# Sliding-window attention feeding a mixture of eight experts: q and k held eight tokens to a partition instead of six, the decay mask computed on the chip, and the second and third batch loaded and turned in another order

## The chip, the cores and the metric

The kernel runs on one core of a Trainium2 chip. The metric is the device time of one execution, in microseconds. PE is the matrix engine, PEld its weight loads, DVE the vector engine, ACT the scalar engine, POOL the general engine (here it mostly issues converting DMAs), SP the engine that issues plain DMAs.

## The reference, cut to what matters

```python
# q, k, v: (8 batches, 8 heads, 576 tokens, 64), float32
scores = q @ k.T / 8
rel    = pos[:, None] - pos[None, :]
mask   = (rel >= 0) & (rel < 128)
scores = where(mask, scores - slope[h] * abs(rel), -1e9)     # slope[h] = 2 ** -(h + 1)
x      = softmax(scores) @ v          # (4608 tokens, 512)
P      = exp(x @ w_gate)              # (4608, 8 experts)
for _ in range(8):                    # Sinkhorn: rows, then columns
    P /= P.sum(1); P /= P.sum(0); P *= 4608 / 8
out    = sum(P[:, e:e+1] * (relu(x @ w1[e]) @ w2[e]) for e in range(8))   # w1 512x1024, w2 1024x512
```

## The kernel before, in words

**Loading and turning.** All inputs are float32 in memory and become float16 on the way in, so they come through POOL's queue. `load_qk(b)` (L159) issues four loads for a batch, k and q of heads 0 to 3 and of heads 4 to 7, into tiles `kf`, `qf` with a ring of four buffers. `RT` is 6: a partition holds six consecutive tokens, 96 partitions hold the 576. `turn` (L184) reorders such a tile on DVE into `kp` or `qp`, and `tr_unit` (L194) transposes one pair of heads: `RT` PE transposes of 96 columns each into PSUM (`psT`), then one copy that puts the tokens back into their natural order, on ACT for k (`KT`, L208) and on DVE for q (`QT`, L213). `load_v` (L172) brings v of a batch in five pieces into `vsb_80` or `vsb_81`.

**Attention.** A batch has five key blocks (`kb` 0 to 4; 128 tokens, the last 64), so there are 40 blocks. For each half of the heads `scores` (L218) makes the scores of a key block against up to 256 queries on PE (`psS`), ACT takes the exponential (`pt`, L238), and DVE multiplies by the decay mask (L246). The mask `maskT` is a 512 KB constant (head by 256 queries) that SP's queue loads at the start (L363). The block after it, `attend` (L255) multiplies by v (`psN`), DVE normalises into `xsb` (L286, L287), and `put_x` (L313) transposes that into `xT`. `gates` makes the gate logits.

**Order.** All of it is written out by hand under a manual schedule, so each engine runs its list in order. The loop is at L406. Units of `tr_unit` for the next batch are spread over a block; the loop says when:

```python
                if b == 0:
                    if kb >= 3:
                        units = [(1, nm, 2 * kb - 6 + n) for n in (0, 1) for nm in ("k", "q")]
                elif kb >= 1 and b + 1 < B:
                    units = [(b + 1, nm, kb - 1) for nm in ("k", "q")]
```

For batch 0 the next batch is turned at the ends of `kb` 2 and 3; for every other batch `turn(b + 1, ..., "k")` stands ahead of the first mask of `kb` 0 and 2. Expert 0 needs no routing weight before it is scaled, so its work for the first 24 of 36 token blocks is mixed into the attention loop: `fill` takes pieces of it (L117 first layer, L135 second layer) at 2.85 per block, from the first 512 finished tokens on.

**After the attention.** The Sinkhorn loop (L485) runs on DVE and POOL while PE does the remaining first-layer work of expert 0. Then come expert 1 (nine units of 512 tokens, the loop at L904, `h` 0 to 8) and the experts 2 to 7 in pairs, with Strassen products in both layers (`l1_product` L653, `Unit.product` L760). In expert 1's units `set_apart` (L526) scales a quarter of expert 0's result into a tile `c` (L532) and stores it to `out` through `store_from` (L69, L73) on SP. The tile comes from a ring `st` of five buffers that also serves `m5` (L688) and the staging tiles of `gather_far` (L780, L781); ACT's write of the next `c` waits until both stores of the one before have landed. In the last pass `put_row` (L810) stores finished rows, `add_out` (L817) adds a block's second half into `out` by an accumulating DMA of POOL, and the last unit stores its last rows from ACT's and SP's queues. Loads of later experts' weights (1 MB each as float16) are issued by POOL, the first two in units 1 and 2 of expert 1.

Of the kernel before, what the change touches and what calls it, by code (L numbers as in the profile page):

```python
# [9 lines left out]
FP16 = mybir.dt.float16  # L10
# [4 lines left out]
def kernel(  # L15
# [20 lines left out]
    P = 128  # L36
# [4 lines left out]
    GT = 512  # L41
    NG = Ntok // GT
    NPR = H // 2
    RT = 6
    RATE = 2.85
    RP = S // RT
    scale = float(1.0 / np.sqrt(Dh))

    slopes = 2.0 ** (-8.0 * (np.arange(H, dtype=np.float64) + 1.0) / H)
    _tok = np.arange(2 * P)  # L50
    _kr = np.arange(P)[:, None, None]
    _jq = _tok[None, None, :]
    _rel = _jq - _kr
    maskT_np = np.where(
        (_rel >= 0) & (_rel < P), np.exp(-slopes[None, :, None] * _rel), 0.0
    ).astype(np.float16)
    maskT_h = nc.inline_tensor(maskT_np, name="maskT_c")
    identf_h = nc.inline_tensor(np.eye(P, dtype=np.float32), name="identf_c")
    ident_h = nc.inline_tensor(np.eye(P, dtype=np.float16), name="ident_c")

# [5 lines left out]
    def acc(blk: int):  # L66
        return acc_lo[:, blk, :] if blk < NHI else accs[1][:, blk - NHI, :]

    def store_from(t, blk: int, c0: int, c1: int, engs=(nc.sync,), **kw):  # L69
        n = P // len(engs)  # L70
        for c, eng in enumerate(engs):
            t0 = P * blk + n * c
            eng.dma_start(out=out[t0 : t0 + n, c0:c1], in_=t[n * c : n * c + n], **kw)  # L73

    def store(blk: int, c0: int = 0, c1: int = HD, engs=(nc.sync,)):
        store_from(acc(blk)[:, c0:c1], blk, c0, c1, engs)

    P_sb = per.tile([P, NBLK, E], FP32, name="P_sb")
# [9 lines left out]
    def load_w1(e: int, pool, parts: int = 1):  # L88
        w1ts[e] = pool.tile([P, NDT, Fd], FP16, name=f"w1t_{e}", tag=f"w1{e % 3}", bufs=1)
        w1v = moe_w1[e].rearrange("(dt p) f -> p dt f", p=P)  # L90
        n = Fd // parts
        for c in range(parts):
            nc.gpsimd.dma_start(
                out=w1ts[e][:, :, n * c : n * c + n], in_=w1v[:, :, n * c : n * c + n]
            )
# [50 lines left out]
    with (  # L146
# [12 lines left out]
        def load_qk(b: int):  # L159
            for half in range(2):  # L160
                h0 = 4 * half
                for nm, src in (("k", k), ("q", q)):
                    t = asb.tile(
                        [RP, 4, RT * Dh], FP16, name=f"{nm}f_{b}_{half}", tag="qkf", bufs=4
                    )
                    nc.gpsimd.dma_start(
                        out=t,
                        in_=src[b, h0 : h0 + 4].rearrange("h (p r) d -> p h (r d)", r=RT),
                    )
                    raw[(nm, b, half)] = t  # L170

        def load_v(b: int, kbs=range(NKB)):  # L172
            vsb = vsbs[b % 2]
            for kb in kbs:
                k0 = kb * P
                nk = min(P, S - k0)
                nc.gpsimd.dma_start(  # L177
                    out=vsb[0:nk, kb, :, 0:Dh],
                    in_=v[b, :, k0 : k0 + nk, :].rearrange("h s d -> s h d"),
                )  # L180
# [13 lines left out]
        def tr_unit(b: int, nm: str, j: int):  # L194
            jj = j % 2
            tt = turned[nm]
            psT = aps.tile([P, RT, RP], FP16, name=f"psT_{nm}_{b}_{j}", tag="pmm", bufs=4)
            for r in range(RT):
                nc.tensor.matmul(  # L199
                    out=psT[:, r, :],  # L200
                    lhsT=tt[:, r, 2 * Dh * jj : 2 * Dh * jj + 2 * Dh],
                    rhs=ident[0:RP, 0:RP],
                    is_transpose=True,
                    start=(r == 0),
                    stop=(r == RT - 1),
                )
            if nm == "k":
                nc.scalar.copy(  # L208
                    out=KTs[b % 2][:, j, :].rearrange("p (i r) -> p i r", r=RT),
                    in_=psT.rearrange("p r i -> p i r"),  # L210
                )
            else:
                nc.vector.tensor_copy(  # L213
                    out=QTs[b % 2][:, j, :].rearrange("p (i r) -> p i r", r=RT),
                    in_=psT.rearrange("p r i -> p i r"),
                )

        def scores(b: int, kb: int, half: int):  # L218
# [141 lines left out]
        with tc.manual_schedule():  # L360
            nc.sync.dma_start(out=ident, in_=ident_h.ap())
            load_qk(0)
            nc.sync.dma_start(out=maskT, in_=maskT_h.ap())  # L363
            for vsb in vsbs:
                nc.vector.memset(vsb[:, :, :, Dh : Dh + 2], 1.0)
            load_v(0, range(NKB - 1))
            load_w1(0, per, 2)
            nc.gpsimd.dma_start(
                out=wg_sb, in_=moe_w_gate.rearrange("(dt p) e -> p dt e", p=P)
            )  # L370
            load_v(0, range(NKB - 1, NKB))
            load_qk(1)
            load_w2(0, per)
            load_v(1)

            blocks = [(b, kb) for b in range(B) for kb in range(NKB)]
            pts: dict = {}
            groups = 0
            turn(0, 0, "k")
            turn(0, 0, "q")  # L380
            for j in range(2):
                tr_unit(0, "k", j)
                tr_unit(0, "q", j)

            def finish(i: int):
                b, kb = blocks[i]
                return attend(b, kb, pts[i], pts[i - 1] if kb > 0 else None)

            def finish2(i: int, xsb):
                nonlocal groups  # L390
                b, kb = blocks[i]
                put_x(b, kb, xsb)
                done = b * S + min(S, (kb + 1) * P)
                while (groups + 1) * GT <= done:
                    nc.sync.dma_start(
                        out=x_dram(groups), in_=xT[:, :, GT * groups : GT * groups + GT]
                    )
                    if groups in (NHI // 4, NHI // 4 + 1):
                        load_x(f"0_{groups}", groups)
                    add_group(groups)  # L400
                    groups += 1
                return done

            xsbs: dict = {}
            done = 0
            for i, (b, kb) in enumerate(blocks):  # L406
                units = []
                if b == 0:
                    if kb >= 3:
                        units = [(1, nm, 2 * kb - 6 + n) for n in (0, 1) for nm in ("k", "q")]  # L410
                elif kb >= 1 and b + 1 < B:
                    units = [(b + 1, nm, kb - 1) for nm in ("k", "q")]
                credit = min(credit + RATE, 6.0) if groups else 0.0
                pt0, mask0 = scores(b, kb, 0)
                if i == 0:
                    turn(0, 1, "k")
                    turn(0, 1, "q")
                    for j in range(2, 4):
                        tr_unit(0, "k", j)
                        tr_unit(0, "q", j)  # L420
                if i > 2:
                    gates(done)
                if i > 1:
                    done = finish2(i - 2, xsbs.pop(i - 2))
                for u in units[: len(units) // 2]:
                    tr_unit(*u)
                fill(1)
                turning = kb in (0, 2) and 0 < b < B - 1
                if turning:
                    turn(b + 1, kb // 2, "k")  # L430
                mask0()
                pt1, mask1 = scores(b, kb, 1)
                pts[i] = (pt0, pt1)
                if i > 0:
                    xsbs[i - 1] = finish(i - 1)
                mask1()
                fill(2)
                for u in units[len(units) // 2 :]:
                    tr_unit(*u)
                fill(1)  # L440
                if turning:
                    turn(b + 1, kb // 2, "q")
                if b == 0 and kb in (2, 3):
                    turn(1, kb - 2, "k")
                    turn(1, kb - 2, "q")
                if kb == 0 and b >= 1 and b + 1 < B:
                    load_v(b + 1)
                if kb == 3 and b + 2 < B:
                    load_qk(b + 2)
            i = len(blocks) - 1  # L450
            credit = 1e9
            xsbs[i] = finish(i)
            gates(done)
            done = finish2(i - 1, xsbs[i - 1])
            fill(2)
            gates(done)
            done = finish2(i, xsbs[i])
            fill(1 << 20)
            gates(done)
# [7 lines left out]
    with (  # L467
# [348 lines left out]

        def add_out(blk):  # L817
            store_from(
                acc(blk)[:, HF:HD], blk, HF, HD, (nc.gpsimd,), accum_op=ALU.add
            )  # L820

        def make_x(j, part):
# [265 lines left out]
```

## Time and profile before

| | |
|---|---|
| median of three runs | 1035.37 us (1033.54 to 1036.13) |
| the profiled execution: its time, its span | 1036.13 us, 1034.4 us |
| granted clock | 0.995 |
| PE, PEld busy | 999.3 us (97%), 810.6 us (78%) |
| DVE, ACT, POOL busy | 825.2 us (80%), 647.8 us (63%), 214.6 us (21%) |
| DMA | 128.06 MB; POOL's queue 60.58 MB, 42.9% of 16 engines' span; SP's 65.79 MB, 20.1% |

The busy time of PE in some stretches (us from the span's start):

| stretch | PE busy | DVE | ACT | what runs |
|---|---|---|---|---|
| 0 to 10 | 1.13 | 1.44 | 1.92 | first loads |
| 10 to 20 | 6.47 | 6.11 | 5.59 | batch 0 |
| 20 to 30 | 8.21 | 8.02 | 5.65 | batch 0, second batch turned |
| 30 to 40 | 7.59 | 6.75 | 4.98 | end of batch 0, begin of batch 1 |
| 40 to 50 | 9.81 | 7.16 | 6.32 | batch 1, first work of expert 0 |
| 50 to 60 | 10.00 | 5.87 | 6.30 | the same |
| 200 to 220 (20 us) | 17.77 | 14.82 | 9.00 | Sinkhorn |
| 1020 to 1035 (15 us) | 8.70 | 8.56 | 0.00 | last sums and stores |

In the lines of the timeline a row gives the start, the duration, the engine, the line, the operation, output<-input, the shapes, the count, and in brackets how long the engine stood idle before it and what ended that. Rows of several like instructions are merged. A matmul's end is modelled, so its pitch is read from the starts. SPq, ACTq and POOL rows of DMA_DIRECT2D are issues, not transfers.

### The profile page before, as it was taken

What the parts mean: (1) busy time and instruction counts of PE and PEld (TensorE: products, weight loads), DVE (VectorE), ACT (ScalarE), POOL (GpSimd) and SP (SyncE); (2) the same over time, 40 slices, a digit from 0 to 9 for tenths busy, and PEclk for the clock granted to TensorE, in tenths of its full rate; (3) what the DMA queues carried; (4) which work ended last, traced back from release to release, by engine and by line L of the source; (5) the groups of instructions that cost most, each with busy time, mean ns of one, the idle gap of its engine ahead of it and who ended that gap; (6) DMA issues with size and microseconds to landing.
All of it is one profiled execution on the core that took longest, in us unless ns stands there. A gap on an engine that the chain in (4) does not pass through costs nothing. (4 is left out here: it accounts for less than half of the span.)

```text
span 1034.4 us, 22423 instructions
## 1 busy us (share of the span) xinstructions
PE 999.3 (97%) x9195; PEld 810.6 (78%) x9195; DVE 825.2 (80%) x1282; ACT 647.8 (63%) x1176; POOL 214.6 (21%) x224
## 2 busy tenths in 40 slices
PE   4899999899999999999999999999999999999997
PEld 2555555445888878888888888888888888888886
DVE  4766666576899978877888998888789988888886
ACT  4576767556999856655666656666556665565652
POOL 6332230020322321111112211111111112222222
PEclk9999999999999999999999999999999999999999
DMA  9978893193697794434336964344446635555546
GB/s 177 186 93 99 113 100 54 61 193 102 149 206 154 149 181 102 113 93 93 92 93 133 181 127 101 93 106 110 103 101 136 132 93 133 134 142 148 140 103 133
DMA packets 127078, 128.06 MB, mean 124 GB/s; under 512 B 44128, under 2 KB 104704, under 8 KB 126976
## 3 DMA queue, kind: packets, MB, share of 16 engines
q0 software_dynamic: 94784, 60.58, 42.9%
q1 hardware_dynamic: 31872, 65.79, 20.1%
q8 instruction: 72, 1.18, 0.4%
q10 hardware_dynamic: 320, 0.26, 0.1%
q14 instruction: 30, 0.25, 0.1%
HBM read 113.62 MB, written 16.66 MB: 126 GB/s over the span
## 5 line engine op out<-in xcount | busy, mean ns | idle before, releaser
L117 PEld LDWEIGHTS <-w1t_100 128*128 128x128 f16 x288 | 27.1, 101 | 28.7 <-issue 5.4
L653 PEld LDWEIGHTS <-w1t_3233 128*128 128x128 f16 x288 | 28.1, 98 | 5.9 <-issue 2.5
L653 PEld LDWEIGHTS <-w1t_3215 128*128 128x128 f16 x288 | 28.2, 98 | 5.8 <-issue 1.3
L653 PEld LDWEIGHTS <-w1t_7818 128*128 128x128 f16 x288 | 28.2, 98 | 5.4 <-issue 2.1
L653 PEld LDWEIGHTS <-w1t_7989 128*128 128x128 f16 x288 | 28.1, 98 | 4.3 <-issue 0.3
L653 PEld LDWEIGHTS <-w1t_5152 128*128 128x128 f16 x288 | 28.2, 98 | 3.7 <-issue 0.3
L653 PEld LDWEIGHTS <-w1t_10754 128*128 128x128 f16 x288 | 28.2, 98 | 3.6 <-issue 0.3
L653 PEld LDWEIGHTS <-w1t_3970 128*128 128x128 f16 x256 | 25.0, 98 | 2.9
L177 POOL DMA_DIRECT2D vsb_81<-in_v_dram x20 | 17.3, 871 | 25.4 <-PE psN_4_885 L278 5.2
L177 POOL DMA_DIRECT2D vsb_80<-in_v_dram x20 | 17.6, 889 | 17.9 <-PE psN_4_1287 L278 5.6
L230 PEld LDWEIGHTS <-KT_76 64*128 64x128 f16 (+1 forms) x160 | 6.0, 100 | 15.8 <-issue 13.3
L497 POOL PARTITION_ALL_REDUCE ca_sb<-cs_sb x8 | 3.2, 395 | 63.1 <-DVE cs_sb L494 63.1
L230 PEld LDWEIGHTS <-KT_77 64*128 64x128 f16 (+1 forms) x160 | 5.3, 97 | 13.8 <-issue 12.6
L539 ACT ACTIVATE acc_lo<-acc_lo,Pe_sb 128x512 f32<-128x512 f32 (+1 forms) x24 | 14.8, 615 | 0.0
L73 POOL DMA_DIRECT2D out_dram<-acc_lo x12 | 13.5, 1526 | 0.0
L303 PEld LDWEIGHTS <-xT 128*128 128x128 f16 x144 | 6.1, 98 | 7.4 <-issue 4.9
L781 POOL DMA_DIRECT2D acc_lo<-st_1_0_3813 x1 | 1.2, 1243 | 37.3 <-ACT st_1_0_3813 L780 37.3
L199 PE MATMUL psT_k_0_124<-ident,kp_0_120 96*128 96x96 f16 x6 | 0.7, 278 | 8.2 <-DVE kp_0_120 L188 8.2
L653 PEld LDWEIGHTS <-ws_1_3529 128*128 128x128 f16 x72 | 6.9, 97 | 1.7 <-DVE xd_0_3537 L612 0.6
L653 PEld LDWEIGHTS <-ws_2_4288 128*128 128x128 f16 x72 | 7.0, 98 | 1.5 <-issue 0.7
L808 DVE TENSOR_TENSOR acc_lo<-acc_lo 128x512 f32<-128x512 f32 x12 | 7.7, 684 | 0.0
L73 POOL DMA_DIRECT2D out_dram<-acc_hi x6 | 5.7, 1575 | 9.7 <-DVE acc_hi L771 9.7
(4167 smaller groups left out, 3574.7 us busy)
## 6 DMA issues: line engine op xcount, KB each, us to landing
xTd<-xT SPq DMA_DIRECT2D x9, 512.0 KB, 3.2
out_dram<-acc_lo SPq DMA_DIRECT2D x12, 256.0 KB, 5.7
vsb_80<-in_v_dram POOLq DMA_DIRECT2D x16, 128.0 KB, 7.8
vsb_81<-in_v_dram POOLq DMA_DIRECT2D x16, 128.0 KB, 4.4
out_dram<-acc_lo SPq DMA_DIRECT2D x12, 128.0 KB, 4.6
out_dram<-acc_lo POOLq DMA_DIRECT2D x12, 128.0 KB, 7.5
w1t_100<-in_moe_w_dram POOLq DMA_DIRECT2D x2, 512.0 KB, 10.9
w2t_113<-in_moe_w_dram POOLq DMA_DIRECT2D x1, 1024.0 KB, 14.1
```

What stands on the lines that cost most here:

```text
L73: eng.dma_start(out=out[t0 : t0 + n, c0:c1], in_=t[n * c : n * c + n], **kw)
L117: nc.tensor.matmul(out=psh, lhsT=w1t[:, dt, P * ft : P * ft + P], rhs=x[:, dt, :], start=(dt == 0), stop=(dt == NDT - 1),)
L177: nc.gpsimd.dma_start(out=vsb[0:nk, kb, :, 0:Dh], in_=v[b, :, k0 : k0 + nk, :].rearrange("h s d -> s h d"),)
L199: nc.tensor.matmul(out=psT[:, r, :], lhsT=tt[:, r, 2 * Dh * jj : 2 * Dh * jj + 2 * Dh], rhs=ident[0:RP, 0:RP], is_transpose=True, start=(r ...
L230: nc.tensor.matmul(out=ps[0:nk, hh, jj, 0:nq], lhsT=KT[rows, 2 * half + jj, k0 : k0 + nk], rhs=QT[rows, 2 * half + jj, k0 : k0 + nq],)
L303: nc.tensor.matmul(out=psG, lhsT=xT[:, dt, P * blk : P * blk + P], rhs=wg_sb[:, dt, :], start=(dt == 0), stop=(dt == NDT - 1),)
L497: nc.gpsimd.partition_all_reduce(ca_sb, cs_sb, P, bass_isa.ReduceOp.add)
L539: nc.scalar.mul(acc(blk)[:, c], acc(blk)[:, c], Pe_sb[:, 0, blk : blk + 1])
L653: nc.tensor.matmul(out=ps[:, f, :], lhsT=a[:, kt, f0 : f0 + P], rhs=b[:, kt, :], start=(m in (1, 5) and f == 0 and kt == 0), stop=(kt == 1 ...
L781: nc.gpsimd.dma_start(out=quad(self.g, rh, ch), in_=st, accum_op=ALU.add)
L808: tt(out=t, in0=t, in1=quad(g, 1, 1), op=ALU.add)
```

## The change

- `RT` is 8: a partition holds eight consecutive tokens, 72 partitions hold a batch, a unit is eight PE transposes of 72 columns. k is put back into natural order as before. q is not: within 64 tokens, position 8r + i holds token 8i + r, so that its copy reads and writes runs of eight elements. The mask, `xT`, the results and the rows of `acc` follow that order, and every store to `out` undoes it: its destination is a pattern of 8 by 8 rows, and a store of 128 rows becomes two of 64.
- The 512 KB mask is gone. A 64 KB table of distances (60000 outside the window) is loaded, and ACT makes the mask from it by eight exponentials of 128 x 256, four after the first half's exponential of the first block and four after the second's.
- At the start the order on POOL's queue is v of batch 0 whole, the gate weights, q and k of batch 1, expert 0's first layer, v of batch 1, expert 0's second layer (before: v of batch 0 but for its last piece, expert 0's first layer, the gate weights, the last piece, q and k of batch 1, second layer, v of batch 1).
- Batch 2 is turned during batch 1 as batch 1 is during batch 0: `turn` at the ends of `kb` 2 and 3, units in `kb` 3 and 4.

```diff
-    RT = 6
+    RT = 8
+    HB = 64
+    NHB = S // HB
+    HI = HB // RT
...
+    _pos = np.arange(2 * P)
+    _tok = (_pos // HB) * HB + (_pos % HI) * RT + (_pos % HB) // HI
+    _rel = _tok[None, :] - np.arange(P)[:, None]
+    rel_np = np.where((_rel >= 0) & (_rel < P), _rel, 60000.0).astype(np.float16)
...
-    def store_from(t, blk: int, c0: int, c1: int, engs=(nc.sync,), **kw):
-        n = P // len(engs)
+    def store_from(t, blk: int, c0: int, c1: int, engs=(nc.sync, nc.sync), **kw):
         for c, eng in enumerate(engs):
-            t0 = P * blk + n * c
-            eng.dma_start(out=out[t0 : t0 + n, c0:c1], in_=t[n * c : n * c + n], **kw)
+            t0 = P * blk + HB * c
+            eng.dma_start(
+                out=out[t0 : t0 + HB, c0:c1].rearrange("(i r) d -> r i d", r=RT),
+                in_=t[HB * c : HB * c + HB],
+                **kw,
+            )
...
-                    out=QTs[b % 2][:, j, :].rearrange("p (i r) -> p i r", r=RT),
-                    in_=psT.rearrange("p r i -> p i r"),
+                    out=QTs[b % 2][:, j, :].rearrange("p (c r i) -> p r c i", r=RT, i=HI),
+                    in_=psT.rearrange("p r (c i) -> p r c i", i=HI),
...
-            nc.sync.dma_start(out=maskT, in_=maskT_h.ap())
+            rel = asb.tile([P, 2 * P], FP16, name="rel")
+            nc.sync.dma_start(out=rel, in_=rel_h.ap())
+            def make_mask(half):
+                for h in range(4 * half, 4 * half + 4):
+                    nc.scalar.activation(
+                        out=maskT[:, h, :], in_=rel, func=AF.Exp, scale=-float(slopes[h])
+                    )
...
-            load_v(0, range(NKB - 1))
-            load_w1(0, per, 2)
+            load_v(0)
...
-            load_v(0, range(NKB - 1, NKB))
             load_qk(1)
+            load_w1(0, per, 2)
+            load_v(1)
             load_w2(0, per)
-            load_v(1)
...
-                if b == 0:
+                late = b < 2
+                if late:
                     if kb >= 3:
-                        units = [(1, nm, 2 * kb - 6 + n) for n in (0, 1) for nm in ("k", "q")]
+                        units = [(b + 1, nm, 2 * kb - 6 + n) for n in (0, 1) for nm in ("k", "q")]
...
                 if i == 0:
+                    make_mask(0)
...
                 pt1, mask1 = scores(b, kb, 1)
+                if i == 0:
+                    make_mask(1)
...
-                turning = kb in (0, 2) and 0 < b < B - 1
+                turning = kb in (0, 2) and not late and b < B - 1
...
-                if b == 0 and kb in (2, 3):
-                    turn(1, kb - 2, "k")
-                    turn(1, kb - 2, "q")
+                if late and kb in (2, 3):
+                    turn(b + 1, kb - 2, "k")
+                    turn(b + 1, kb - 2, "q")
...
-                acc(blk)[:, HF:HD], blk, HF, HD, (nc.gpsimd,), accum_op=ALU.add
+                acc(blk)[:, HF:HD], blk, HF, HD, (nc.gpsimd, nc.gpsimd), accum_op=ALU.add
```

## The prediction

> **What bounds the kernel now.** I read the page first, then busy time by stretches, then the timeline of the start, of expert 1 and of the end. PE is busy 97% of the span, and from 45 to 200 us its waits on other engines add up to about 4.5 us, and PE is full again from 204 on. So a change can act at the start, where PE has nothing to do, on PE's own work, by a new stall of PE later, and at the end.
>
> ```profile
> 7.44 0.67 DVE L188 COPY kp_0_120<-kf_0_85 96x1536 f16<-96x1536 f16 x1 [6.41 <-DMA kf_0_85<-in_k_dram]
> 8.91 0.56 DVE L188 COPY qp_0_122<-qf_0_87 96x1536 f16<-96x1536 f16 x1 [0.80 <-DMA qf_0_87<-in_q_dram]
> 11.19 0.76 DVE L213 COPY QT_78<-psT_q_1_148 128x576 f16<-128x576 f16 x1 [0.20 <-PE psT_q_1_148 L199]
> 12.43 1.02 ACT L238 ACTIVATE pt_0_0_161<-psS_0_0_156 128x1024 f16<-128x1024 f32 x1 [1.08 <-PE psS_0_0_156 L230]
> 13.35 0.63 ACT L208 COPY KT_76<-psT_k_2_167 128x576 f16<-128x576 f16 x1
> 15.84 1.02 ACT L238 ACTIVATE pt_0_1_205<-psS_0_1_200 128x1024 f16<-128x1024 f32 x1 [1.08 <-PE psS_0_1_200 L230]
> 17.56 1.02 ACT L238 ACTIVATE pt_1_0_213<-psS_1_0_208 128x1024 f16<-128x1024 f32 x1 [0.70 <-PE psS_1_0_208 L230]
> ...
> 35.61 0.42 DVE L327 COPY xT<-psXT_3_471 128x512 f16<-128x512 f16 x1 [0.36 <-PE psXT_3_471 L318]
> 38.14 0.56 DVE L188 COPY kp_0_478<-kf_0_369 96x1536 f16<-96x1536 f16 x1 [2.11 <-DMA kf_0_369<-in_k_dram]
> 38.62 0.68 DVE L246 TENSOR_TENSOR pt_0_0_463<-pt_0_0_463,maskT 128x1024 f16<-128x1024 f16 x1
> 40.97 1.91 PE L117 MATMUL psh_0_0_545<-xT,w1t_100 128*128 128x512 f16 x4
> ```
>
> The timeline of the start: everything waits for the first k and q (7.44, 8.91); two exponentials follow each other at 1.72 us, as scores and exponential share one PSUM tile; from 23.7 to 36 DVE has gaps of 1.7 us in all; at 36.0 it stands 2.11 us for batch 2's k, with the mask of the running block behind that turn. At 40.97 expert 0's work begins and PE is full from there.
>
> **The first loads.** The 512 KB mask landed 3.7 us after its issue at 1.13, beside the first k. From 7.44 on one 288 KB load lands per 1.4 to 1.7 us. Taking 448 KB away is worth at most 448/288 x 1.5 = 2.3 us, at least nothing; I take 1.0, as the mask and k moved side by side only until 4.8. The turn of q grows: 1536 elements take 0.55, and 2048 at the same rate 0.55 x 2048/1536 = 0.73 at most, so +0.13 to +0.18. The q copy reads and writes runs of eight like the xT copy (512 elements in 0.42) instead of single elements (576 in 0.76): 0.42 x 576/512 = 0.47, so -0.29, or nothing if runs of eight are not enough; I take -0.29, the nearer row by access. The first exponential starts 1.0 - 0.15 + 0.29 = 1.1 earlier.
>
> **The mask on ACT.** No row shows it. A 256-element exponential of 64 partitions takes 0.38 (pt_4), a 256-wide ACT operation read from SBUF as here 0.50 (L532); with the 0.10 that neighbours overlap, 0.28 to 0.40 each, a group of four 1.1 to 1.6. I take the upper, nearer row. The first group stands ahead of the copy of k (13.35), and ACT had only 1.08 idle before 15.84; the second ahead of 17.56, where it had 0.70. Together 3.2 less what was idle, 1.8, is 1.4 of delay (0.4 with the short row). The start up to 17.56 thus gains 1.1 + 0.29 (the second pair's copy) - 1.4 = 0.
>
> **Batch 1's turn.** Between 24 and 35 DVE does four turns (+0.15 each) and four q copies (-0.29 each): -0.6 on the chain, 0 to -1.0. Loading q and k of batch 1 ahead of w1 gains nothing: no row of 25.17 to 30.91 waits for them. It delays w1 by four loads, some 6 us, and w1 was down at 21, wanted at 40.97: covered. Without cover each microsecond would be one.
>
> **Batch 2 turned late.** DVE's 2.11 of waiting and the 0.56 of the turn go. Next late is rden_4, which needs psN_4, done on PE at 38.0: the mask can run at 36.0, rden_4 at 38.2 instead of 39.22, so 1.0 is gained. The unit psT_k_0 (0.46 on PE) leaves the stretch too, and comes back where PE is twice as fast. Together 1.6 (1.0 to 2.5). In key blocks 3 and 4 of batch 1 four units follow in a block instead of two; ACT's exponentials there are 0.81 and 0.38 instead of 1.02, so ACT has room: nothing, at worst 1.0. POOL's loads of batch 3 wait for those turns, until some 57 instead of 52; loads then landed in 4 to 5 us and DVE wants them at 61.8: covered.
>
> **PE's own work.** 64 units of eight 72-column transposes for six of 96. Warm, six of 96 columns start 0.04 apart (98.57 to 98.84 with the next row), and 65-column products of attend 0.031 (four in 0.125). 72 columns give 0.031 to 0.040, so 0.25 to 0.32 for 0.24: 64 x 0.01 = +0.6, at most 5. I take the 65-column row.
>
> **The stores.** Twice as many DMAs of half the rows. In the timeline of expert 1:
>
> ```profile
> L73 SPq DMA_DIRECT2D out_dram<-c_2_3914 x2: 338/338/338, 273.5 to 279.4; - x2
> ...
> DMA to landing us min/median/max: 5.8/7.7/9.6
> ```
> ```profile
> 284.79 0.50 ACT L539 ACTIVATE acc_lo<-acc_lo,Pe_sb 128x256 f32<-128x256 f32 x1
> 285.29 0.51 ACT L532 ACTIVATE c_3_4098<-acc_lo,Pe_sb 128x256 f32<-128x256 f32 x1
> ...
> 288.29 0.57 ACT L684 COPY lb_3_1_4145<-la_3_1_4140 128x512 f32<-128x512 f32 x1
> 288.80 1.23 DVE L593 TENSOR_TENSOR xl_4044<-xl_4044,Pb_4_4046 128x1024 f16<-128x1024 f16 x1 [0.71 <-DMA Pb_4_4046<-PTd]
> ```
>
> The store issued at 279.4 landed 5.8 later, at 285.2, and ACT's write of c_3, which waits for it, starts at 285.29, where the 0.4 pitch of its neighbours would allow 285.19. While the 1 MB weight loads run there is no slack. PE takes the next lb product at 288.91, right after ACT's copy ends at 288.86. SP's queue holds the x and Pb loads behind the store, and DVE already waits for Pb. Behind c_2's store the x load landed 2.1 later and Pb 1.4 after it (287.3, 288.7), so one more DMA in this queue costs 1.4 to 2.1. ACT's stall is then 1.4 at c_3, and 0.8 at c_4 (0.6 of slack); of each 0.25 is idle time. PE loses about 2.0; at least 0 (bytes are the same), at most twice the 5.8 that a store takes now, less cover: 6. The other units' stores land in 1.7 to 5.0 with 5.5 to spare.
>
> The Trainium skill (DMA: Bandwidth & Descriptors, section "Why a DMA increments its semaphore by 16 and not by 1") says that a transfer uses the largest number of engines up to 16 that divides the slowest dimension on both sides, on SP's and ACT's queues the lowest-numbered ones. By it an 8 by 8 store runs on 8 engines, so that both halves burden the same ones, and this term and the next would be nearer 4 and 1.6; no run here shows it yet.
>
> **The end.**
>
> ```profile
> 1028.78 2.75 ACTq L73 DMA_DIRECT2D out_dram<-acc_hi  x4
> 1029.08 0.69 DVE L771 TENSOR_TENSOR acc_hi<-acc_hi,M_6_8_13897 128x512 f32<-128x512 f32 x1 [0.33 <-PE M_6_8_13897 L760]
> ```
>
> The last eight stores were of 64 rows before and stay so, landing in 2.0 to 2.2. Ahead of them on SP two stores become four: 2 x 0.43 of issue, against 0.4 of free time, so SP is 0.4 later. Two accumulating stores of POOL become four: 1.71 of issue becomes at most 3.4, ending 1029.0, and with 4.9 to land 1033.9, inside the span. I take +0.8, from 0 to 2.5 (one more landing of 2.2).
>
> **Sum.** 0 - 0.6 - 1.6 + 0.6 + 2.0 + 0.8 = +1.2. The profiled execution took 1036.13 (span 1034.4 and 1.73 around it), 0.76 above the median; 1037.3 there is 1036.5 as a median. About 0.3%, 3.1 us, is what a measurement of this kernel can tell from no change.
>
> PE also starts cold: the four products of psh_0_0 take 1.91, from 46 on 1.02, while the granted clock reads 1.00. The switch came at 45.4, and I let it move with the start. The Trainium skill (TensorE: Matmul & The Clock Gate, section "Part 1: The HAM clock gate") has a free-running window of 3.4 us decide it; that would put up to 1.7 us either way on the sum.
>
> **Rivals.** A: as summed, the start's gain is handed back by stores, 1036.5, within 0.3%; chance 0.45 with all its mixtures. B: the start's bounds come true, stores stay hidden. Loads 2.3 earlier instead of 1.0, masks short (1.0 less), DVE -1.0, late turning -2.5: 0 - 1.3 - 1.0 - 1.0 - 2.5 + 0.6 = -5.2, 1030.2. For it: gaps of PE until 41 are real. Against: the mask group on ACT sits in the very chain. 0.20 for faster by over 3.1. C, the other side: stores in expert 1. If the second store lands 4 us later instead of 1.4, ACT is late at c_3 and c_4 by 4 + 3.4, PE by 6, the end by 2.5: -2.2 + 0.6 + 6 + 2.5 = +6.9, 1042.3. It decides from some 3 us of extra landing time on. For it: 285.2 against 285.29; against: only two of nine units run beside a weight load. 0.35. That the change doesn't do what it says (q and k of 72 partitions landing no earlier) takes 1.0 off the gain: 1037.5, within A.
>
> The range reaches into B and C: 1031.5 to 1042.0; A's own is 1033.5 to 1039.5.
>
> **What would show it.** First k at 6.4, first q at 7.9; q copies of 0.47; mask exponentials of 0.50; no DVE wait for batch 2; expert 0's first piece near 39; ACT waiting before c_3 and c_4 and nowhere else in expert 1. Wrong if first exponentials are no earlier, if PE's pitch of 72 columns is 0.040, or if PE has new waits after 300.

## Result and the profile after

The changed kernel takes 1043.43 us (median; 1042.68 to 1044.20), the kernel before, on the same chip, 1035.68: a ratio of 1.0079 (95% interval 1.0062 to 1.0096), 7.8 us slower. The forecast of 1036.5 and its range, up to 1042.0, are both missed. The profiled execution took 1042.68, its span is 1040.8. (The ratio is worked out from the single runs; that of the two medians is 1.0075.)

The start of the kernel after, from the timeline:

```profile
6.34 0.69 DVE L192 COPY kp_0_121<-kf_0_85 72x2048 f16<-72x2048 f16 x1 [5.30 <-DMA kf_0_85<-in_k_dram]
8.68 0.91 DVE L192 COPY qp_0_123<-qf_0_87 72x2048 f16<-72x2048 f16 x1 [1.65 <-DMA qf_0_87<-in_q_dram]
11.31 0.46 DVE L217 COPY QT_78<-psT_q_1_155 128x576 f16<-128x576 f16 x1 [0.50 <-PE psT_q_1_155 L203]
12.25 1.02 ACT L242 ACTIVATE pt_0_0_170<-psS_0_0_165 128x1024 f16<-128x1024 f32 x1 [0.79 <-PE psS_0_0_165 L234]
13.17 1.32 ACT L372 ACTIVATE maskT<-rel 128x256 f16<-128x256 f16 x4
18.42 1.01 ACT L242 ACTIVATE pt_1_0_238<-psS_1_0_233 128x1024 f16<-128x1024 f32 x1
...
40.39 1.89 PE L121 MATMUL psh_0_0_574<-xT,w1t_111 128*128 128x512 f16 x4
```

k comes 1.10 earlier, as forecast, but q only 0.23 earlier (8.68 after 8.91), and its turn takes 0.91 instead of the forecast 0.68 to 0.73. So the first exponential starts 0.18 earlier instead of 1.1, and with four mask exponentials ahead of it in 1.32 the third one starts 0.86 later than before. Still, expert 0 begins 0.58 earlier. These are two single profiles, and the first loads scatter: the first k is turned between 6.55 and 8.60 us in the six profiles below and above that load the 512 KB mask, and between 6.29 and 6.54 in the nine with the front of after. So the directions hold over more profiles, the hundredths don't: the third exponential starts at 17.42 to 18.71 in the six (median 17.6) and at 18.12 to 18.80 in the nine (18.3).

Expert 1, timeline. The first two rows are of before, the others of after:

```profile
336.56 1.22 DVE L593 TENSOR_TENSOR xl_4781<-xl_4781,Pb_8_4783 128x1024 f16<-128x1024 f16 x1
339.62 0.60 PE L653 MATMUL lb_7_1_4880<-xl_4597,w1t_3215 128*128 128x256 f16 x4
```
```profile
285.08 0.49 ACT L547 ACTIVATE c_3_4241<-acc_lo,Pe_sb 128x256 f32<-128x256 f32 x1
...
337.56 1.22 DVE L608 TENSOR_TENSOR xl_4932<-xl_4932,Pb_8_4934 128x1024 f16<-128x1024 f16 x1 [1.05 <-DMA Pb_8_4934<-PTd]
340.59 0.60 PE L668 MATMUL lb_7_1_5032<-xl_4746,w1t_3352 128*128 128x256 f16 x4 [0.95 <-DVE lc_7_1_5061 L708]
...
361.40 1.23 DVE L608 TENSOR_TENSOR xl_5303<-xl_5303,Pb_0_5305 128x1024 f16<-128x1024 f16 x1 [1.20 <-DMA Pb_0_5305<-PTd]
365.02 0.60 PE L668 MATMUL lb_0_1_5378<-xl_5118,w1t_3370 128*128 128x256 f16 x4 [1.35 <-DVE lc_0_1_5403 L708]
```

ACT's write of c_3, where the forecast put its wait, shows no idle time ahead of it. Instead DVE waits for the Pb loads, at 337 and 361, and each time PE waits for DVE right behind: 0.95 us at the first place (339.62 became 340.59) and 1.35 at the second.

The end: the issue queues of SP (before, then after) and of ACT (after), from the timelines of those engines, each of one row, start and length in us:

```profile
1017.23 13.99 SPq L73 DMA_DIRECT2D out_dram<-acc_hi  x14
```
```profile
1018.74 19.03 SPq L73 DMA_DIRECT2D out_dram<-acc_hi  x24
```
```profile
1030.92 6.61 ACTq L73 DMA_DIRECT2D out_dram<-acc_hi  x4
```

The last sum, on DVE, which was at 1029.08, and SP's stores from `acc_hi` as the answer on that tile lists them (issue time min/median/max in ns, first and last start), before and then after:

```profile
L73 SPq DMA_DIRECT2D out_dram<-acc_hi x14: 332/433/597, 1017.2 to 1030.7; - x14
```
```profile
1030.59 0.69 DVE L786 TENSOR_TENSOR acc_hi<-acc_hi,M_6_8_14100 128x512 f32<-128x512 f32 x1 [0.33 <-PE M_6_8_14100 L775]
```
```profile
L73 SPq DMA_DIRECT2D out_dram<-acc_hi x24: 596/603/1471, 1018.7 to 1037.0; - x24
```

The issue is the time that a queue takes to hand a DMA over; the landing is counted from the start of the issue until the data have arrived. The list of DMA issues between 1012 and 1045 us gives the median landing as its last number, before and then after:

```profile
out_dram<-acc_hi POOLq DMA_DIRECT2D x6, 128.0 KB, 4.9
out_dram<-acc_hi SPq DMA_DIRECT2D x6, 128.0 KB, 2.2
```
```profile
out_dram<-acc_hi SPq DMA_DIRECT2D x16, 64.0 KB
out_dram<-acc_hi POOLq DMA_DIRECT2D x12, 64.0 KB, 5.1
```

For the stores of after on SP it gives none, so a median over all stores of `acc_hi` (2.3 before, 5.0 after, 5.2 in e6) sets mostly SP's stores against POOL's alone and says nothing of SP. The expectation of e6 below takes its 5.0 and 2.3 from there. The trace does hold the updates of each store's semaphore, 16 for a store of before and nine for one of after, and the last of them is the landing. By these SP's 14 stores of before land in 1.7 to 3.5 us (median 2.2), its 24 of after in 2.5 to 5.6 (median 3.6).

In before SP's last store is issued 1.7 us after the last sum begins, in after 6.4 us. One issue has become 0.60 instead of 0.43 at the median, there are 24 instead of 14, and a store lands in 3.6 instead of 2.2. From the start of the last sum to the span's end it was 5.3 us and is now 10.2; the last sum itself is 1.5 us late.

The table of stretches shows what the DMA engines moved (the last three columns are granted clock, DMA share, GB/s); before, then after:

```profile
1028.00:1032.00 4.00, 1.04 (x10) 0.68 (x7) 1.40 (x3) 0.00 (x0) 0.00 (x0) 0.97 0.92 203
1032.00:1036.00 4.00, 0.00 (x0) 0.00 (x0) 0.00 (x0) 0.00 (x0) 0.00 (x0) 0.50 0.11 28
```
```profile
1028.00:1032.00 4.00, 2.55 (x24) 2.04 (x21) 2.58 (x4) 0.00 (x0) 2.66 (x3) 1.00 0.60 122
1032.00:1036.00 4.00, 0.00 (x0) 0.00 (x0) 0.00 (x0) 0.00 (x0) 0.00 (x0) 0.97 0.69 165
1036.00:1040.00 4.00, 0.00 (x0) 0.00 (x0) 0.00 (x0) 0.00 (x0) 0.00 (x0) 0.50 0.40 128
```

Before, the end ran at a DMA share of 0.92 and 203 GB/s and was over by 1032.7. After, it stays at 0.4 to 0.7 and 122 to 165 GB/s until 1039.4. (The share adds up the packets' times and reads 1.74 between 10 and 20 us, so it isn't a measure of how full the engines are.) The queue packets on the page speak of the same halving: ACT's queue, which carries only the four 64-row stores of the end.

```profile
q10 hardware_dynamic: 320, 0.26, 0.1%
```
```profile
q10 hardware_dynamic: 288, 0.26, 0.1%
```

320 is four times 64 rows and 16 completions, 288 four times 64 and 8. That, and the nine semaphore updates instead of 16, agree with the rule of the Trainium skill that the forecast named and set aside (DMA: Bandwidth & Descriptors, "Why a DMA increments its semaphore by 16 and not by 1"): the 8 by 8 pattern runs on 8 engines here.

### The profile page after: what moved, and what is told of

Same layout as the page of the kernel before. It is cut to its first block, busy times and chain, and to the rows that moved or that the text cites. A ratio compares the mean times of both kernels' runs of the same rounds, so it can differ in the third digit from the quotient of the medians.

```text
span 1040.8 us, 22781 instructions
## 1 busy us (share of the span) xinstructions
PE 1000.0 (96%) x9323; PEld 811.2 (78%) x9323; DVE 821.5 (79%) x1282; ACT 649.7 (62%) x1184; POOL 233.2 (22%) x242
## 5 line engine op out<-in xcount | busy, mean ns | idle before, releaser
L121 PEld LDWEIGHTS <-w1t_111 128*128 128x128 f16 x288 | 26.8, 101 | 27.9 <-issue 4.5
L668 PEld LDWEIGHTS <-w1t_3370 128*128 128x128 f16 x288 | 28.1, 98 | 6.7 <-issue 3.3
L668 PEld LDWEIGHTS <-w1t_3352 128*128 128x128 f16 x288 | 28.2, 98 | 6.1 <-issue 1.7
L668 PEld LDWEIGHTS <-w1t_7973 128*128 128x128 f16 x288 | 28.2, 98 | 5.1 <-issue 1.9
L668 PEld LDWEIGHTS <-w1t_8144 128*128 128x128 f16 x288 | 28.1, 98 | 4.3 <-issue 0.3
L668 PEld LDWEIGHTS <-w1t_5307 128*128 128x128 f16 x288 | 28.1, 98 | 3.7 <-issue 0.3
L668 PEld LDWEIGHTS <-w1t_10909 128*128 128x128 f16 x288 | 28.2, 98 | 3.6 <-issue 0.3
L668 PEld LDWEIGHTS <-w1t_4112 128*128 128x128 f16 x256 | 25.1, 98 | 2.9
L73 POOL DMA_DIRECT2D out_dram<-acc_lo x24 | 24.5, 1829 | 0.0
L73 POOL DMA_DIRECT2D out_dram<-acc_hi x12 | 11.2, 2125 | 6.0 <-DVE acc_hi L786 6.0
L668 PEld LDWEIGHTS <-ws_1_3668 128*128 128x128 f16 x72 | 6.9, 97 | 1.7 <-DVE xd_0_3676 L627 0.6
L668 PEld LDWEIGHTS <-ws_2_4434 128*128 128x128 f16 x72 | 7.0, 98 | 1.5 <-issue 0.7
L668 PEld LDWEIGHTS <-ws_1_3665 128*128 128x128 f16 x72 | 7.0, 98 | 0.8
```

The source lines that it names most:

```text
L73: eng.dma_start(out=out[t0 : t0 + HB, c0:c1].rearrange("(i r) d -> r i d", r=RT), in_=t[HB * c : HB * c + HB], **kw,)
L121: nc.tensor.matmul(out=psh, lhsT=w1t[:, dt, P * ft : P * ft + P], rhs=x[:, dt, :], start=(dt == 0), stop=(dt == NDT - 1),)
L668: nc.tensor.matmul(out=ps[:, f, :], lhsT=a[:, kt, f0 : f0 + P], rhs=b[:, kt, :], start=(m in (1, 5) and f == 0 and kt == 0), stop=(kt == 1 ...
```

## Experiments

A kernel whose stores aren't those that belong to its order of rows writes the rows of `out` in another order than the reference's (e1, e2, e3, e4, e5, e7, e9, e13); computation and bytes are the same. Each ratio is to the kernel before, measured beside it on the same chip, where its median was between 1034.4 and 1035.8. The column "end" is the time from the start of DVE's last sum to the span's end, in the profiled execution.

| kernel | median us | ratio to before, 95% interval | end us |
|---|---|---|---|
| before | 1035.4 | 1 | 5.3 |
| after | 1043.43 | 1.0079 (1.0062 to 1.0096) | 10.2 |
| e1 after, one plain store | 1035.64 | 1.0003 (0.9993 to 1.0013) | 5.3 |
| e2 after, two plain stores | 1039.78 | 1.0043 (1.0027 to 1.0059) | 7.6 |
| e3 after, two stores of 16 by 4 | 1040.63 | 1.0049 (1.0034 to 1.0064) | 7.2 |
| e4 before, stores of after | 1042.97 | 1.0079 (1.0061 to 1.0097) | 11.0 |
| e5 after, last pair plain | 1037.88 | 1.0022 (1.0012 to 1.0032) | 5.9 |
| e6 after, eight stores on ACT's queue | 1041.72 | 1.0063 (1.0050 to 1.0076) | 11.2 |
| e7 after, one store of 8 by 16 | 1038.28 | 1.0028 (1.0018 to 1.0039) | 8.0 |
| e9 as e2, eight stores on ACT's queue | 1037.88 | 1.0027 (1.0017 to 1.0037) | 5.6 |

**e1 to e4: is it the stores, and their number or their engines?**

```diff
 e1: after
-            t0 = P * blk + HB * c                       # two pieces, 8 by 8
+            if engs[0] is engs[1]: engs = engs[:1]      # one plain piece of 128 rows
 e2: after
-                out=out[t0 : t0 + HB, c0:c1].rearrange("(i r) d -> r i d", r=RT),
+                out=out[t0 : t0 + HB, c0:c1],
 e3: after
-                out=out[t0 : t0 + HB, c0:c1].rearrange("(i r) d -> r i d", r=RT),
+                out=out[t0 : t0 + HB, c0:c1].rearrange("(i r) d -> r i d", r=16),
 e4: before, with store_from and add_out of after
```

> The changed kernel with the stores of the kernel before: one DMA of 128 consecutive rows instead of two of 8 by 8 rows. The rows of a block thus go to out in the permuted order; nothing else is left out. Theory ENGINES (a store of 8 by 8 rows runs on half of the DMA engines, these are full at the end, and the last stores queue up): the end shrinks by 4.9 us, the DVE waits for Pb in expert 1 go, 1043.4 - 6 = 1037.5. Theory COUNT (it is the doubled number of DMAs and their longer issue on SP): the same, 1037.5. Theory ELSEWHERE (the loss is in the attention part and the stores only move it): 1042 to 1043.5.

> The changed kernel with two DMAs of 64 consecutive rows for each store; again only the order of the rows in out is left out. ENGINES: all 16 engines again, so within 1 us of one plain store, about 1038. COUNT: the number of DMAs is still doubled, so most of the loss stays, 1042 to 1043.5. ELSEWHERE: 1042 to 1043.5.

> The changed kernel with the row pattern of a store 16 by 4 instead of 8 by 8: the same number of DMAs, of rows and of bytes, scattered rows as before, only the slowest dimension is 16 (the order of the rows in out is then not the token order). ENGINES: 16 engines, so about 1038 to 1039, a little above two plain stores for the longer issue of a three-dimensional pattern (0.60 against 0.34 us each). COUNT and a theory SCATTER (scattered rows in memory are slow): 1042 to 1043.5.

> The kernel before with nothing but the stores of the changed kernel, 8 by 8 rows, two DMAs each; the rows of out are then in another order than the tokens. ENGINES and COUNT: 1035.5 + 6 = 1041.5, most of it behind the last product, the rest as DVE waits for Pb in expert 1. ELSEWHERE: 1035.5 to 1036.5.

With one plain store the rest of the change costs nothing that can be told from nothing (e1; it gives back 7.8 us, where two theories had expected 6), and after's stores alone make before just as slow as after (e4). So the whole loss is the stores. Neither single theory holds: twice the number with all 16 engines costs 4.1 us (e2 less e1), and the 16 by 4 pattern, whose stores have 16 updates too, doesn't differ from it by more than the intervals (e3). The step to 8 by 8 costs some 3 more. SP's landing at the end goes the same way: a median of 2.2 in e1, 2.5 in e2, 2.3 in e3, 3.7 in e4.

**e5: where?**

```diff
+    # put_row, add_out and the end: one plain piece (64 plain rows for the last eight)
+    store_from(acc(blk)[:, c0:c1], blk, c0, c1, engs, plain=True)
```

> After, with the stores of the last expert pair (rows finished at 1016 to 1031 us) put back to one plain piece of 128 rows (the last eight to 64 plain rows), while the c stores in expert 1 stay two pieces of 8 by 8. The stored rows of the last pair are in another order than the reference's. Theory END: of the 7.8 us that the stores cost, about two thirds arise behind the last unit, on SP's queue, and 2.2 us in expert 1, where the x and Pb loads queue behind the c stores: 1037.3 to 1038.3, with the last sum still 1.5 to 2 us late and 5.3 us from its start to the end. Theory EXPERT1: the stores beside the weight loads cost nearly all: 1041 to 1043.

END holds in its time, 1037.88; the last sum is 0.9 us later than in before instead of 1.5 to 2, and the end is 5.9 instead of 5.3. The last pair's stores cost 1043.43 - 1037.88 = 5.5 us, those in expert 1 1037.88 - 1035.64 = 2.2.

**e6 and e9: is it SP's queue, or the landing?**

```diff
                 if unit.last:
-                    put_row(g - 1, 1)
-                    put_row(g - 1, 0)
+                    put_row(g - 1, 1, nc.scalar)        # their stores on ACT's queue
+                    put_row(g - 1, 0, nc.scalar)
```

> After, with the eight stores of the last unit's put_row issued on ACT's queue instead of SP's, same pieces, same bytes, same number in all. Theory ISSUE: the end is late because SP issues 24 stores at 0.60 to 0.64 us each in one unbroken row from 1018.7 on; 16 instead of 24 on SP take 10.2 us and leave it idle before the last sums, so the last store is issued some 4 us sooner: 1038.5 to 1040. Theory LANDING: the stores on 8 of 16 engines land in 5.0 us instead of 2.3 and stores wait for earlier ones to land whichever queue issues them: 1042.5 to 1043.5, as after.

> The kernel with two plain stores of 64 rows (1039.78, all 16 engines) and the eight stores of the last unit's put_row on ACT's queue instead of SP's. Theory ISSUE: with all engines at work the unbroken row of 24 issues on SP is what makes the end late (7.6 us from the last sum to the end instead of 5.3); with 16 on SP the end falls back and only expert 1's 2.2 us are left: 1037.3 to 1038.3. Theory LANDING: stores wait for earlier ones to land on whichever queue: 1039 to 1040, as without the move.

e6's 1041.72 lies between the two ranges, e9's 1037.88 in ISSUE's. The move gains the same with 8 engines and with 16: the ratio falls by 0.0016 (1.7 us) from after to e6 and from e2 to e9, and both times the intervals overlap. The profiled ends differ more (11.2 in e6, 5.6 in e9), but e6's profile is the second slowest of its five runs and e9's the third fastest of twelve. SP's waits in e6, and then in e9 (us in total, times, longest):

```profile
SPq L73 <- DMA out_dram<-acc_hi: 6.2, 2, 4.4
```
```profile
SPq L73 <- DMA out_dram<-acc_hi: 1.7, 2, 1.5
```

The 6.2 us of e6 look like stores that wait for earlier ones to land. For the longer part, 4.4, that is wrong: DVE finishes the row that SP stores next only at 1028.47, and SP goes on 0.21 us later.

```profile
1027.78 0.69 DVE L823 TENSOR_TENSOR acc_hi<-acc_hi 128x512 f32<-128x512 f32 x1
1028.68 0.60 SPq L73 DMA_DIRECT2D out_dram<-acc_hi  x1
```

An earlier store happened to land at 1028.62, in between, and the profile names what came last. (In before SP stands idle for 4.4 us at the same place.) The other 1.8 us is a real wait for a landing, and such waits are in the other kernels too. The program's stores share eight semaphores, and a store is issued only when the one before it on its semaphore has landed. Of SP's last four stores in after, issued at 1034.14, 1035.09, 1036.38 and 1037.03, the last three follow such a landing within 0.1 us. In e2, with 16 engines, the last two do the same (1034.53 and 1035.11). So in both kernels the end isn't one unbroken row of issues: the number of stores and the time that they take to land (2.5 in e2, 3.6 in after) act together. How much of the 5.5 us each of them makes isn't settled.

**e7: half the engines without the double number.**

```diff
-            t0 = P * blk + HB * c                       # two pieces of 8 by 8
+            t0 = P * blk                                # one piece, r=RT: 8 by 16
```

> After, with every 128-row store in one piece, but of 8 rows by 16 (so 8 engines, as in after, with the number of stores of before). The stored rows are in another order than the reference's. With one plain piece it was 1035.64, with two pieces on 16 engines 1039.8 to 1040.6, with two on 8 engines 1043.4. Theory SUM: number and engines add up: 1035.6 + 2.8 = 1038.4 (1037.8 to 1039.2). Theory TOGETHER: halved engines cost only where SP's queue is already full of twice as many issues: 1035.6 to 1036.6.

SUM holds: 1038.28, 2.6 above e1. With e2's 4.1 for the number that makes 6.7 of the 7.8 us. SP's stores land in 4.4 at the median (2.6 to 6.5) instead of 2.2. The issue has changed with the pattern as well, 0.60 instead of 0.43, so by this run the 2.6 isn't shown to be the engines' alone. But e2 and e3 have nearly the same issue time, 0.59, on 16 engines, and their stores land in 2.5 and 2.3: the slow landing goes with the 8 engines and not with the longer issue.

**e13: how do the stores in expert 1 cost 2.2 us?**

```diff
-                        set_apart(h + 1, k // 4)
+                        set_apart(h + 1, k // 4, held if k == 4 else None)
...
                 load_next(h)
+                for t, blk in held:
+                    store_from(t, blk, HF, HD)
```

> The kernel with plain stores in the last pair (1037.88), and in expert 1 the second c store of each unit issued behind the unit's x and Pb loads on SP instead of ahead of them; same stores, two pieces of 8 by 8. Theory QUEUE: the 2.2 us that are left arise because the Pb loads queue behind these stores, so that DVE waits for Pb and PE for DVE (3.4 us of PE waits between 300 and 420 against 0.9 with one plain store): 1035.7 to 1036.5. Theory ENGINES: the eight engines are busy with the stores, whatever stands ahead in the queue: 1037.3 to 1038.2.

1041.42 (ratio 1.0065, 1.0052 to 1.0079, against e5's 1.0022): both theories miss the time. PE's waits between 300 and 420 in e5, and then in e13:

```profile
PE lb L670 <- DVE lc L710: 3.4, 5, 1.2
PE lb L670 <- ACT lb L701: 0.5, 2, 0.3
```
```profile
PE lb L673 <- ACT lb L704: 1.5, 3, 0.8
PE lb L673 <- DVE lc L713: 1.0, 3, 0.4
```

The waits for DVE, and with them those for Pb, fall from 3.4 to 1.0, so their source was what stands ahead of the loads on SP: QUEUE is right on that. The same waits are 0.9 in e1, 3.5 in e2 and 2.4 in e7, so the doubled number is enough for them without 8 engines, and 8 engines add to them without the doubled number. But the stores now come later, and ACT waits where it didn't:

```profile
287.08 0.51 ACT L549 ACTIVATE c<-acc_lo,Pe_sb 128x256 f32<-128x256 f32 x1 [2.58 <-DMA acc_lo<-st]
```

It is the wait that the forecast named, at c_3, in a kernel that issues the second store of a unit later. PE then waits 2.3 us for ACT between 255 and 300, where e5 has no wait, and the loss against e5 arises there. The c tiles share the ring `st` with the staging tiles; the profile names a staging tile's DMA, and which user of the ring ACT waited for isn't settled.

**e8, e10, e12: parts of the change without the stores.**

```diff
 e8:  before + "late = b < 2" of the change (units, turning, turn), nothing else
 e10: before
+                behind = turning and b == 1 and kb == 0
-                if turning:
+                if turning and not behind:
                     turn(b + 1, kb // 2, "k")
...
+                if behind:
+                    turn(b + 1, kb // 2, "k")
 e12: before + rel, make_mask of the change, tokens in plain order
```

> Before, with one part of the change alone: batch 2's k and q turned in key blocks 3 and 4 of batch 1 instead of in block 0 and on, six tokens to a partition, stores and mask as before. Theory FORECAST: the 2.11 us wait of DVE at 36 us goes and the late turns find room: 1.6 us gained, 1034.0 (1033.1 to 1034.6). Theory CROWDED: in after, expert 0 begins 0.6 us sooner, but from its first product to its first second-layer product it takes 16.9 us instead of 15.05, as PE waits for four turns in one block: the gain is handed back, 1035.6 to 1036.6, and that stretch takes 16.5 us or more here too.

1035.36, ratio 0.9995 (0.9986 to 1.0005): between the two ranges, nearer to CROWDED's. The stretch that CROWDED named takes 15.73 us, more than 15.05 but not 16.5. The same PE work in before and e8: the first product of expert 0 at 40.97 and 39.41, so 1.56 earlier (forecast 1.6); the first one of the second layer at 56.02 and 55.14; the third second-layer block at 61.28 and 60.77. So of the 1.56 us that e8 is ahead at the first product, 0.51 are left there. The waits of e8 (first row) and after (second row) on the way:

```profile
54.41 0.43 PE L199 MATMUL psT_k<-ident,kp 96*128 96x96 f16 x6 [0.71 <-DVE kp L188]
```
```profile
56.38 0.43 PE L203 MATMUL psT_k_2_811<-ident,kp_1_780 72*128 72x72 f16 x8 [0.54 <-DVE kp_1_780 L192]
```

A wait of 0.71 for the turn, and one unit more on a PE that is full here: from the first product on before transposes seven of batch 2's eight units and e8 all eight, at 0.26 each; before does the first of them at 40.51, while PE waits anyway. Together that is 0.97 of the 1.05 that went, though the scatter at the start (below) is nearly as large.

> Before, with one edit: in block 0 of batch 1 the turn of batch 2's first k is issued behind both masks, beside that of q, instead of ahead of the first mask; units, stores and everything else as before. Theory PLACE: the 2.11 us wait was in the way of the mask, and what took the gain back in the kernel with the late turns was only the crowd in key blocks 3 and 4; without it expert 0 begins 1.0 to 1.6 us sooner and keeps it: 1034.0 to 1034.8. Theory ABSORBED: a gain at the start is swallowed by later waits on other engines (la_0_0 for the first Pb load, 175 to 217 us): 1035.3 to 1036.

1034.56, ratio 0.9993 (0.9982 to 1.0003). In the direction of PLACE, but the interval doesn't exclude no change. Its first product came 0.35 earlier, too little to tell from the scatter at the start (below).

> Before, with one part of the change alone: the mask from the 64 KB table by ACT's exponentials, in plain token order. Theory FORECAST: the earlier loads (1.0) and the masks on ACT (1.4) leave +0.1 to +0.4 at expert 0's start. Theory CHAIN: in after a group of four took 1.32 us and the third exponential came 0.86 us later than before, as q landed only 0.2 us sooner; masks in the chain of exponentials cost 0.8 to 1.5 us at expert 0's start: 1036.2 to 1037.

1035.05, ratio 0.9999 (0.9988 to 1.0010): the mask alone is worth nothing that can be told, as FORECAST says, and most of CHAIN's 0.8 to 1.5 is excluded. In its profile the first exponential starts 1.24 earlier than in before (11.19), the third 0.42 earlier (17.14), and expert 0 begins 1.0 earlier (39.97), which neither theory had.

**e11 and e14: can a version beat both?**

```diff
 e11: e10 with, at the end (likewise for the columns 0 to HF)
-                    for blk in (4 * g, 4 * g + 1):
-                        store(blk, HF, HD, engs)
+                    store_two(4 * g, HF, HD, engs)      # one DMA for two blocks and 64 rows
 e14: e11 with held stores as in e13
```

> The kernel before it, and the last eight stores (64 rows by 256 columns of one block) joined into four of two blocks each, half the rows on ACT's queue and half on SP's: the last sum's store is then the second issue on each queue instead of the third and fourth. Theory NUMBER: 0.6 us less than without, as one issue of 0.5 to 0.7 us falls away ahead of the end on each queue. Theory BYTES: what counts at the end is that the bytes land, and one store of 128 KB lands as late as two of 64: within 0.2 us of the kernel without.

> Before with the turn of batch 2 behind the masks and the last eight stores joined into four (1033.73), and the second c store of each unit of expert 1 issued behind the x and Pb loads. Theory QUEUE: the c store ahead of the Pb load is also in the way with one plain store of 128 rows (PE waits of 1.3 us between 300 and 420): 0.5 to 1.3 us less, 1032.4 to 1033.2. Theory ENOUGH: the loads have slack with one store: 1033.5 to 1034.2.

e11 takes 1033.73, ratio 0.9987 (0.9974 to 0.9999): the fastest kernel here, by a margin that the interval only just separates from before, which among so many kernels can be chance; its end is 4.95 against 5.27 of e10, some of NUMBER's 0.6, in one profile each. e14 takes 1040.52 (1.0057, 1.0045 to 1.0070), about 7 us above e11: both its theories fall. ACT stands ahead of c there as in e13, up to 2.2 us at a time, and PE waits 3.8 us for ACT between 300 and 420. The place of the second c store behind the loads is worse than ahead of them, with one piece as with two.

## Why the prediction was wrong

- **The end, +0.8 forecast, 5.5 measured (e5).** This step failed. It counted two more issues on SP, with no other store in their way, and allowed, as its bound, one more landing of 2.2. It left out the stores of `put_row` ahead of them: eight become sixteen, at 0.60 instead of the 0.33 to 0.46 of before, and fill the 4.4 us in which SP stood idle before (1022.6 to 1027.0). And it took it that the last stores wait for nothing but their issue, where the runs show them waiting for earlier ones, whose landing is 3.6 at the median instead of 2.2. The last one on SP is issued 6.4 us behind the start of the last sum instead of 1.7, and lands 2.8 later. The sum's price of an issue, 0.43, came from plain stores, and its landing, 2.0 to 2.2, from stores on 16 engines. POOL's accumulating stores, which e5 puts back too, have landed by 1035.3 in after, 4.5 us ahead of SP's last.
- **The engines.** The Trainium skill's rule was set aside because no run showed it. By it the two terms would have been 4 and 1.6, the sum 2.8 higher and the forecast 1039.3: nearer, but the second term still too small by 3.9. e7 gives 2.6 for one store on 8 engines.
- **Stores in expert 1, +2.0 forecast, 2.2 measured (e5 less e1).** The size is right, the place wrong, so the size is luck: c_3 and c_4 had no wait; DVE waited for Pb, which the forecast had seen at 288.80 as already late, and let pass. Its own sign of being wrong came with that: PE waits 4.1 us between 300 and 420 instead of 1.8. Rival C, the chance for slower, came near in its total (1042.3) by this same wrong wait; its mechanism only appears when the stores are issued still later (e13, e14).
- **Batch 2 turned late, -1.6 forecast, -0.5 (-1.4 to +0.5) measured (e8).** The gain came at 40 us as worked out. That it costs the blocks it is moved to nothing failed: the worst case that the forecast allowed, 1.0, is what came back, 1.05, 0.71 of it a wait and 0.26 a unit that PE does in a full stretch instead of a waiting one.
- **The start, 0 forecast.** Its sum fits the mask by itself (e12). In e12 the first exponential comes 1.24 earlier and the third 0.42; in after these are 0.18 earlier and 0.86 later, as q landed only 0.2 earlier, not 1.0. What holds q back there wasn't tested. Four mask exponentials take 1.32, between the forecast's 1.1 and 1.6.
- **Batch 1's turn, -0.6.** q copies take 0.46 (forecast 0.47). The gain isn't between 24 and 35: from the second reciprocal (L286, 23.72 in before) to the xT copy at 35.61 it is 11.89 us in before and 12.02 in after. It comes later: between two equal first-layer products, at 68.38 and 122.73 in before, PE needs 54.35 us in all profiles with six tokens (before, e8, e10, e12) and 53.42 in those with eight (after, e1, e7, e9). That the shorter q copies make these 0.93 us is likely but wasn't tested by itself.
- **PE's own work, +0.6 forecast, nothing seen.** A unit's PE row has 0.42 with six and with eight transposes, and two units start 0.26 apart in both.
- **Sum without the stores.** -1.6 forecast, +0.3 (-0.7 to +1.3) measured by e1.

The clock at the start: the second product group of expert 0 takes 1.79 at 43.78 in before and 1.02 at 43.65 in e4, whose front is the same, while the granted clock reads 1.00 in both. From the first group to the fourth it is 7.4 us in before and 6.5 in e4. e10 and e11 too have one front between them, and expert 0 begins at 40.62 and 39.69. So single profiles that differ by less than 0.9 us at the start say nothing, and the starts of e8, e10 and e12 are read with that in mind. The Trainium skill's window of 3.4 us (TensorE: Matmul & The Clock Gate, "Part 1: The HAM clock gate") isn't contradicted; no run here tests it.

## What to carry to other kernels

Cost a store by the queue that issues it: number times issue time, from where that queue last stood idle to the end, and the last store goes behind that row. Then ask which earlier store it waits for, and how long that one takes to land. Before making a destination pattern, look at the slowest dimension: with 8 by 8 half of the engines were left, and the landing went from 2.5 (e2) to 3.6 with the same number of stores. Look at what a median is taken over: a landing of 5.0 was POOL's stores, not SP's. And when a wait is put down to a DMA, look whether the data were ready before it landed. A step that is moved from a waiting stretch of PE into a full one costs its own PE time there, and a wait where it is crowded.

## What was not expected of the hardware

- A store's issue on SP takes 0.33 to 0.46 for 128 plain rows (before; 0.34 for 16 of the 18 in expert 1), and 0.60 for 64 rows as 8 by 8 (median 0.603 in after), also for 128 rows as 8 by 16 (0.604 in e7): the bytes don't set it.
- 64 plain rows are no cheaper to issue than 128: 0.594 at the median in e2, 0.433 in before (over all 14).
- Stores on half of the engines land later: at the median 3.6 instead of 2.5 with 24 stores on SP (after, e2), 4.4 instead of 2.2 with 14 (e7, e1).
